# One-bank instead of two-bank PSUM tiles in the second layer, and a fold's seven combinations beside one tile

## The chip, the cores and the metric

One core of a Trainium2 chip runs the whole program. The metric is device time in microseconds; the kernel before takes 1497.6 us, the median of 3 runs (1495.95 to 1499.32).

## The reference

```
attention twice, per batch and head: packed = attn(p, k, v); x = attn(q, packed, packed)
    B = 8, H = 8, S = 576, head 64, 32 packed tokens;  x becomes 4608 x 512
xn  = x / rms(x) * rms_g
y   = (silu(xn @ w_gate) * (xn @ w_val)) @ w_out      512 -> 1536 -> 512
a, b = y @ w1, y @ w2                                 512 -> 1024 each
out = ((a * b) @ w3) @ w_out2                         1024 -> 1024 -> 512
```

Inputs and outputs are 32-bit floats.

## The kernel before

Every 32-bit operand of a matmul is split into two parts, a rounded high part and the rest (`split`, L54 to L56: ScalarE copies, VectorE or GpSimd subtracts), and each product is made as three matmuls: high by high, high by low, low by high. 

The program runs in stages. Attention and the dense gate and value layer come first and leave the activations transposed in device memory (hT_d). Then nine *y tiles* of 512 tokens each multiply them by w_out (`y_part`, L549 to L568). A y tile has 12 steps; in each, SP issues the load of a slice hr four steps ahead, ScalarE and VectorE split a slice two steps ahead into hh and hl, and TensorE does 12 matmuls into four PSUM banks. At the end four evictions and two stores (y_d) follow. Tiles alternate between two sets of banks, "gv" and "at".

Beside the y tiles run two other pieces of work, cut into small steps by Python generators. `fold_parts` (L665 to L695) takes w3 @ w_out2, which `folded` has made on TensorE into the tiles w34o, and makes seven combinations of its four blocks: each is one `put`, that is a ScalarE copy and a VectorE subtraction of 128 x 1024 and a store, some with additions on GpSimd. `layer2` (L634 to L642) rounds the blocks of w1 and w2 (`converting`; c_h and c_y are ScalarE's copies, lines 108 and 109) and makes seven combinations of each of four groups (`group`), stored to ws_d. `together` (L407 to L420) spreads such generators over the steps of the y tiles: each has a number of calls, and a start and an end as shares of the stage; at most one call, that of the one furthest behind, goes with each step, and whatever is left of a generator is run at the end in one go. Stores are held back by some steps (`store_later`, `stores`, L349 to L356) and issued on SP, in whose queue the loads of hr stand as well. `fetch_y` loads the first token block for the second layer.

The second layer works on five pairs of token blocks, three of 512 and two of 384 tokens wide. Each 2 x 2 block product is made by a scheme of seven products instead of eight, so that one step has 7 products x 6 = 42 matmuls, into four accumulators ta, tb, tc and td (`step`, L841 to L890). The order of the products is ta, tb, tc, then ta, tb again, td, tc again. In between, ScalarE copies ta to p1 (a tile named hr, L867), VectorE makes u2 and u3 from tb and p1, c22 from tc and u3, s1 from td and u3 times ta, and the last u2 from tc (the helper `dve` at L839; u2 and c22 are the two halves of a tile named uc, s1 is a tile named s), and GpSimd multiplies u2 by c22 (L883) and makes differences. A pair has 8 steps. Even steps put the four accumulators in four one-bank tiles "gv", odd steps in two two-bank tiles "at", ta and tb in the first, tc and td in the second:

```
def slot(tag):                                                   # L48
    return ps.tile([128, 2, 512], F32, tag=tag, name=tag, bufs=2)
def bank():                                                      # L51
    return ps.tile([128, 512], F32, tag="gv", name="gv", bufs=4)
def four(tag):
    if tag == "gv":
        return [bank() for _ in range(4)]
    return [t[:, j, :] for t in (slot("at"), slot("at")) for j in range(2)]
```

After the 8 steps of a pair comes its output product (`run`, L915 to L985): 28 units of 6 matmuls (L951), each unit three matmuls into the accumulators `acc[0]` in "gv" and three into `acc[1]` in "at", with the same seven-product scheme and the same VectorE and ScalarE reads between. Weights come in tiles of 1024 or 768 KB with four buffers; taking one issues the load of the next (`load_w`, `next_w`, L748 on, issue at L756). All eight PSUM banks are in use: four for "gv", four for "at". The order of instructions on an engine is the order in which the program writes them; tiles and semaphores decide only who waits.

Of the kernel before, what the change touches and what calls it, by code (L numbers as in the profile page):

```python
# [8 lines left out]
F32 = mybir.dt.float32  # L9
# [23 lines left out]
def packed_attention_swiglu_bilinear(ctx: ExitStack, tc, qT, kT, v, pT, rms_g, w_gv, w_out,  # L33
                                     w1, w2, w3T, w_out2, out):
    nc = tc.nc
    PSUM = bass.MemoryType.PSUM
# [8 lines left out]
    y_d = dram.tile([NT // TT, 128, 4, TT], F32, name="y_d")  # L45
    ws_d = [dram.tile([8, 128, 2, n, 2, 128], F32, name=f"ws{n}_d") for n in (3, 4)]

    def slot(tag):  # L48
        return ps.tile([128, 2, 512], F32, tag=tag, name=tag, bufs=2)

    def bank():  # L51
        return ps.tile([128, 512], F32, tag="gv", name="gv", bufs=4)
# [346 lines left out]
    def some(gen, n):  # L399
        for _ in range(n):  # L400
            yield next(gen, None)
# [5 lines left out]
    def together(main, total, *others, most=1):  # L407


        done, taken = 0.0, [0] * len(others)  # L410
        for c in main:
            done += c / total
            late = [n * (done - a) / (z - a) - taken[i] if taken[i] < n else 0.0
                    for i, (n, _, a, z) in enumerate(others)]
            for i in sorted(range(len(others)), key=lambda j: -late[j])[:most]:
                if late[i] > 0:
                    next(others[i][1], None)
                    taken[i] += 1
        for _, gen, _, _ in others:
            drain(gen)  # L420
# [128 lines left out]
    def y_part(t, tag):  # L549
        acc = four(tag)  # L550
        for kk in range(NF):
            n = NF * t + kk
            fetch_h(n + 4)
            split_h(n + 2)
            hi, lo = hts.pop(n)
            for m in range(4):
                for a, (w, x) in enumerate(((wo_h, hi), (wo_h, lo), (wo_l, hi))):
                    nc.tensor.matmul(acc[m], lhsT=w[:, kk, 128 * m:128 * m + 128], rhs=x,  # L558
                                     start=(kk == 0 and a == 0), stop=(kk == NF - 1 and a == 2))
            if kk < NF - 1:  # L560
                stores()
                yield 1.0
        for h in range(2):
            y = yp.tile([128, 2, TT], F32, tag="y", name="y", bufs=2)
            for m in range(2):
                evict(y[:, m], acc[2 * h + m], m)
            store_later(3, out=y_d[t, :, 2 * h:2 * h + 2], in_=y)
        yield 1.0  # L568
# [141 lines left out]
    def fetch_y(p):  # L710
        if p < len(pairs):
            ys[p] = []
            row, w = pairs[p]
            for r in (row, row + w):
# [8 lines left out]

    second = layer2()
    third = fold_parts()
    together(y_part(4, "at"), 12.0, (6, some(second, 6), 0.5, 1.0), (5, some(third, 5), 0.0, 0.9))
    together(chained(y_part(5, "gv"), y_part(6, "at"), y_part(7, "gv")), 36.0, (31, second, 0.0, 0.9),
             (3, third, 0.0, 0.15),
             (1, (fetch_y(0) for _ in range(1)), 0.3, 0.4))

    flush()
# [93 lines left out]
             (3, first_w(), 0.3, 0.8))  # L825
    flush()
    wo_ctx.close()
    p3 = ctx.enter_context(tc.tile_pool(name="p3", bufs=1, side="left"))
    sides = {n: p3.tile([128, 4, TT], F32, name=n) for n in ("s11", "s21", "s12", "s22", "t1s", "t2s", "t4s")}
    OPER = {0: "s11", 4: "t1s", 5: "t2s", 1: "s21", 6: "s12", 3: "t4s", 2: "s22"}  # L830
# [10 lines left out]
    def step(p, n):  # L841
        w = width(p)
        i = LAYER[n]
        half, k = divmod(i, 4)
        xh, xl = xs[p]

        def side(name):
            return sides[name][:, k, :w]

        def prod(t, j, start):  # L850
            pos = ORDER.index(j)
            wi, pos, n = (wa, pos, 3) if pos < 3 else (wb_, pos - 3, 4)
            wi = wi[:, :512 * n].rearrange("p (r j s n) -> p r j s n", r=2, j=n, s=2)
            at = 0
            for a, x in ((0, xh), (1, xh), (0, xl)):
                for r in range(2):
                    nc.tensor.matmul(t, lhsT=wi[:, r, pos, a], rhs=x[:, j, r, :w],  # L857
                                     start=(start and at == 0), stop=(at == 5), skip_group_check=True)
                    at += 1

        ta, tb, tc_, td = (t[:, :w] for t in four("at" if n % 2 else "gv"))
        p1, u3, uc = tmp()[:, :w], tmp()[:, :w], two()
        u2, c22 = uc[:, 0, :w], uc[:, 1, :w]
        s1, s2 = (side("s21"), side("s22")) if half else (side("s11"), side("s12"))
        wa = next_w()
        prod(ta, 0, True)
        nc.scalar.activation(out=p1, in_=ta, func=AF.Copy)  # L867
        prod(tb, 5, True)
        dve(u2, tb, p1)
        prod(tc_, 4, True)  # L870
        yield
        wb_ = next_w()
        prod(ta, 1, False)
        prod(tb, 6, False)
        dve(u3, tb, p1)
        dve(c22, tc_, u3)
        yield
        prod(td, 3, True)
        dve(s1, td, u3)
        dve(s1, s1, ta, ALU.mult)  # L880
        prod(tc_, 2, False)
        dve(u2, tc_, u2)
        nc.gpsimd.tensor_tensor(out=s2, in0=u2, in1=c22, op=ALU.mult)  # L883
        if half == 0:
            diff(side("t1s"), s2, s1, nc.gpsimd)
        else:
            diff(side("t2s"), s2, side("t1s"), nc.gpsimd)
            diff(side("s12"), s2, side("s12"), nc.gpsimd)
            diff(side("t4s"), s1, side("t2s"), nc.gpsimd)
        yield  # L890
# [24 lines left out]
    def run(p):  # L915
        w = width(p)
        ahead = splitting(p, AHEAD)
        diffs = early(p + 1)
        for n in range(8):
            for part, _ in enumerate(step(p, n)):  # L920
                if part in EARLY.get(n, ()):
                    next(ahead)
                if n == 1 and part == 0:
                    fetch_y(p + 1)
                if n in (4, 5) and part == 1:
                    next(diffs, None)
        xs.pop(p)
        drain(ahead)
        drain(diffs)
        later = splitting(p, LATER)  # L930
        sum_ = sums(p + 1)
        acc = [[t[:, :w] for t in four(tag)] for tag in ("gv", "at")]
        p1, u2, u3, c22 = [], [], [], []
        out_stores = []

        def keep(m, half, side, o):
            out_stores.append(dict(out=out[256 * half + 128 * m:256 * half + 128 * m + 128,
                                           pairs[p][0] + side * w:pairs[p][0] + side * w + w], in_=o))

        BANK = {0: 0, 1: 0, 5: 1, 6: 1, 4: 2, 2: 2, 3: 3}  # L940
        for a, j in enumerate(PROD):
            wi = next_w().rearrange("p (s i n) -> p s i n", s=2, i=4)
            last = {0: 1, 5: 6, 4: 2}.get(j, j) == j
            for k in range(4):
                for _ in range(ISSUE[4 * a + k]):
                    next(later, None)
                hi, lo = his.pop((j, k))
                for m in range(2):
                    t = acc[m][BANK[j]]
                    for n, (s, x) in enumerate(((0, hi), (1, hi), (0, lo))):  # L950
                        nc.tensor.matmul(t, lhsT=wi[:, s, k, 128 * m:128 * m + 128], rhs=x,  # L951
                                         start=(j in (0, 5, 4, 3) and k == 0 and n == 0),
                                         stop=(k == 3 and n == 2), skip_group_check=True)
                if k == 1:
                    next(sum_, None)
                if out_stores:
                    nc.sync.dma_start(**out_stores.pop(0))
            for m in range(2):
                ta, tb, tc_, td = acc[m]
                if j == 0:  # L960
                    p1.append(tmp()[:, :w])
                    nc.scalar.activation(out=p1[m], in_=ta, func=AF.Copy)
                elif j == 5:
                    uc = two()
                    u2.append(uc[:, 0, :w])
                    c22.append(uc[:, 1, :w])
                    dve(u2[m], tb, p1[m])
                elif j == 1:
                    c11 = tmp()[:, :w]
                    nc.scalar.activation(out=c11, in_=ta, func=AF.Copy)  # L970
                    keep(m, 0, 0, c11)
                elif j == 6:
                    u3.append(tmp()[:, :w])
                    dve(u3[m], tb, p1[m])
                    dve(c22[m], tc_, u3[m])
                    keep(m, 1, 1, c22[m])
                elif j == 3:
                    dve(u3[m], td, u3[m])
                    keep(m, 1, 0, u3[m])
                elif j == 2:  # L980
                    dve(u2[m], tc_, u2[m])
                    keep(m, 0, 1, u2[m])
        drain(sum_)
        for x in out_stores:
            nc.sync.dma_start(**x)  # L985
# [34 lines left out]
```

## Time and profile before

| | |
|---|---|
| median of 3 runs | 1497.6 us |
| the profiled execution | 1496.0 us |
| its span, first to last instruction | 1494.2 us |
| mean granted TensorE clock | 0.984 |
| TensorE busy | 1360.8 us, 91% |
| VectorE busy | 871.6 us, 58% |
| ScalarE busy | 576.5 us, 39% |
| GpSimd busy | 607.0 us, 41% |
| the nine y tiles and the folding end, and layer 2 starts, at | 865.5 us |

A busy share is the share of the span in which the engine worked on an instruction. The granted clock is the part of full speed at which TensorE was allowed to run: 1.00 is 2.4 GHz, 0.5 is 1.2 GHz.

### The profile page before, as it was taken

Reading aid. Unit: us, or ns where it says so; the run is one execution under the profiler, and the core shown is the slowest. Engines: PE = TensorE matmul, PEld = TensorE weight load, DVE = VectorE, ACT = ScalarE, POOL = GpSimd, SP = SyncE. Lnnn points to the kernel's source line nnn. Section 1 sums busy time; section 2 is a strip of 40 time slices with the busy share of each in tenths; the row PEclk is TensorE's granted clock in tenths of the full one; section 3 lists DMA queues with packets and bytes.
Section 4 is the critical chain, followed back from the end, with each engine's and each line's share of the span. In section 5 each row is a group of like instructions: output and inputs, shape, how many; then the busy total and the mean of one; then the engine's idle time right before and its main releaser. Section 6 shows DMA issues by size and latency. Waiting matters only on the chain.

```text
span 1494.2 us, 23206 instructions
## 1 busy us (share of the span) xinstructions
PE 1360.8 (91%) x8800; PEld 1119.2 (75%) x8800; DVE 871.6 (58%) x1356; ACT 576.5 (39%) x1141; POOL 607.0 (41%) x524
## 2 busy tenths in 40 slices
PE   4579999999999999999899998998889889988888
PEld 2368888888888888888788776776667667878778
DVE  4786576676675577364786734654573447346344
ACT  3465554554556665252555410240042015014013
POOL 2455544545555622022344232452335326235233
PEclk9689999999999999999999999999999999999999
DMA  9844544433213577344899764465447545756654
GB/s 298 302 172 129 188 145 155 160 121 125 104 72 131 182 262 241 100 159 132 309 349 395 261 230 150 169 213 224 155 169 238 178 162 190 269 205 223 226 211 155
DMA packets 82080, 293.55 MB, mean 196 GB/s; under 512 B 9008, under 2 KB 14128, under 8 KB 68016
## 3 DMA queue, kind: packets, MB, share of 16 engines
q1 hardware_dynamic: 81968, 292.07, 56.4%
q8 instruction: 69, 1.13, 0.3%
q14 instruction: 43, 0.35, 0.1%
HBM read 219.68 MB, written 72.35 MB: 195 GB/s over the span
## 4 chain that ended last, share of the span: by engine, by line
PE 72%; DVE 13%; ACT 4%; DMA 3%; issue 3%; SPq 1%; POOL 0%; DVEq 0%; ACTq 0%; POOLq 0%
PE gv L376 17%; PE at L857 12%; PE gv L857 10%; PE at L558 9%; PE at L951 5%; PE gv L951 5%; PE gv L558 4%; PE gv L654 3%; DVE hr L839 3%; DVE uc L839 2%; PE at L337 2%; DMA w<-in_w_dram 1%; DMA hr<-hT_d 1%; PE at L292 1%; DVE s L839 1%
## 5 line engine op out<-in xcount | busy, mean ns | idle before, releaser
L388 POOL TENSOR_TENSOR ht<-th,vl 128x288 f32<-128x288 f32 x192 | 163.6, 861 | 166.7 <-ACT vl L387 79.3
L857 PE MATMUL at<-xh,w 128*128 128x512 f32 (+1 forms) x560 | 146.2, 383 | 56.1 <-DVE uc L839 28.1
L376 PE MATMUL gv<-ah,wbh 128*128 128x288 f32 x768 | 178.0, 313 | 7.3 <-DVE th L383 4.7
L883 POOL TENSOR_TENSOR s<-uc 128x512 f32<-128x512 f32 (+1 forms) x40 | 48.5, 1214 | 313.8 <-DVE uc L839 313.8
L376 PE MATMUL gv<-al,wbh 128*128 128x288 f32 x768 | 166.8, 298 | 0.0
L857 PEld LDWEIGHTS at<-xh,w 128*128 128x128 f32 x560 | 98.9, 189 | 90.2 <-DVE uc L839 35.7
L376 PEld LDWEIGHTS gv<-ah,wbh 128*128 128x128 f32 x768 | 122.3, 190 | 58.5 <-issue 22.8
L376 PE MATMUL gv<-ah,wbl 128*128 128x288 f32 x768 | 165.0, 296 | 0.0
L114 POOL TENSOR_TENSOR c_o<-c_o,c_y 128x512 int32<-128x512 int32 x52 | 74.4, 1431 | 173.0 <-DVE c_o L112 152.3
L857 PE MATMUL gv<-xh,w 128*128 128x512 f32 (+1 forms) x560 | 140.4, 372 | 3.4 <-DVE uc L839 2.2
L56 DVE TENSOR_TENSOR hl<-hr,hh 128x512 fp32r<-128x512 f32 x108 | 98.9, 919 | 49.5 <-ACT hh L55 49.3
L376 PEld LDWEIGHTS gv<-al,wbh 128*128 128x128 f32 x768 | 124.7, 190 | 1.0 <-DVE al L56 0.6
L376 PEld LDWEIGHTS gv<-ah,wbl 128*128 128x128 f32 x768 | 124.3, 190 | 0.0
L857 PEld LDWEIGHTS gv<-xh,w 128*128 128x128 f32 x560 | 101.4, 188 | 23.5 <-DVE uc L839 11.0
L383 DVE SCALAR_TENSOR_TENSOR th<-th,gv 128x288 f32<-128x288 f32 x192 | 84.4, 445 | 55.9 <-ACT th L382 52.1
L558 PE MATMUL at<-hl,wo_h 128*128 128x512 f32 x288 | 112.6, 391 | 2.3 <-DVE hl L56 2.3
L558 PE MATMUL at<-hh,wo_h 128*128 128x512 f32 x288 | 112.4, 390 | 0.2 <-ACT hh L55 0.2
L558 PE MATMUL at<-hh,wo_l 128*128 128x512 f32 x288 | 112.3, 390 | 0.0
L55 ACT ACTIVATE hh<-hr 128x512 fp32r<-128x512 f32 x108 | 67.5, 628 | 97.1 <-PE at L558 49.9
L387 ACT ACTIVATE vl<-gv 128x288 f32<-128x288 f32 x192 | 79.5, 414 | 62.1 <-PE gv L376 58.5
L56 DVE TENSOR_TENSOR wbl<-at,wbh 128x512 fp32r<-128x512 f32 x96 | 66.0, 687 | 61.2 <-ACT wbh L55 60.6
L951 PE MATMUL at<-sh,w 128*128 128x512 f32 (+1 forms) x280 | 83.9, 381 | 13.1 <-DVE uc L839 12.4
(148 smaller groups left out, 2828.0 us busy)
## 6 DMA issues: line engine op xcount, KB each, us to landing
w<-ws_d SPq DMA_DIRECT2D x40, 1024.0 KB, 4.8
w<-w_d SPq DMA_DIRECT2D x35, 1024.0 KB, 4.8
w<-ws_d SPq DMA_DIRECT2D x40, 768.0 KB, 4.4
hT_d<-ht SPq DMA_DIRECT2D x96, 288.0 KB, 2.6
hr<-hT_d SPq DMA_DIRECT2D x108, 256.0 KB, 5.3
w<-in_w_gv_dram SPq DMA_DIRECT2D x24, 512.0 KB, 7.2
w<-in_w_out_dram SPq DMA_DIRECT2D x20, 512.0 KB, 4.8
v<-in_v_dram SPq DMA_DIRECT2D x8, 1152.0 KB, 8.1
```

Source lines behind the costliest of these rows:

```text
L55: nc.scalar.activation(out=hi, in_=src, func=AF.Copy)
L56: eng_lo.tensor_tensor(out=lo, in0=src, in1=hi.bitcast(F32), op=ALU.subtract)
L114: nc.gpsimd.tensor_tensor(out=d, in0=d, in1=shape(y), op=ALU.add)
L376: nc.tensor.matmul(t[:, :HALF], lhsT=w[:, e, 256 * i + 128 * f:256 * i + 128 * f + 128], rhs=x[:, e, HALF * hf:HALF * hf + HALF], start=(n ...
L383: nc.vector.scalar_tensor_tensor(out=th, in0=th, scalar=1.0, in1=t[:, :HALF], op0=ALU.add, op1=ALU.mult)
L387: nc.scalar.activation(out=vl, in_=t[:, :HALF], func=AF.Copy, scale=0.5)
L388: nc.gpsimd.tensor_tensor(out=ht[:, hf], in0=th, in1=vl, op=ALU.mult)
L558: nc.tensor.matmul(acc[m], lhsT=w[:, kk, 128 * m:128 * m + 128], rhs=x, start=(kk == 0 and a == 0), stop=(kk == NF - 1 and a == 2))
L839: nc.vector.tensor_tensor(out=out, in0=a, in1=b, op=op)
L857: nc.tensor.matmul(t, lhsT=wi[:, r, pos, a], rhs=x[:, j, r, :w], start=(start and at == 0), stop=(at == 5), skip_group_check=True)
L883: nc.gpsimd.tensor_tensor(out=s2, in0=u2, in1=c22, op=ALU.mult)
L951: nc.tensor.matmul(t, lhsT=wi[:, s, k, 128 * m:128 * m + 128], rhs=x, start=(j in (0, 5, 4, 3) and k == 0 and n == 0), stop=(k == 3 and n ...
```

## The change

The two-bank "at" tiles move to a PSUM pool of their own, which is closed after the last y tile; from then on the same four banks are four one-bank tiles, for the odd steps of the second layer and for the second accumulator group of the output product. And all seven combinations of the folded weight are made beside the fifth y tile (`y_part(4, ...)`), where five were before and two beside the sixth to eighth.

```diff
+    slots_ctx = ExitStack()
+    slots = slots_ctx.enter_context(tc.tile_pool(name="slots", bufs=1, space=PSUM))
+
     def slot(tag):
-        return ps.tile([128, 2, 512], F32, tag=tag, name=tag, bufs=2)
+        return slots.tile([128, 2, 512], F32, tag=tag, name=tag, bufs=2)
...
-    together(y_part(4, "at"), 12.0, (6, some(second, 6), 0.5, 1.0), (5, some(third, 5), 0.0, 0.9))
+    together(y_part(4, "at"), 12.0, (6, some(second, 6), 0.5, 1.0), (7, third, 0.0, 0.9))
     together(chained(y_part(5, "gv"), y_part(6, "at"), y_part(7, "gv")), 36.0, (31, second, 0.0, 0.9),
-             (3, third, 0.0, 0.15),
              (1, (fetch_y(0) for _ in range(1)), 0.3, 0.4))
...
     wo_ctx.close()
+    slots_ctx.close()
+    pt = ctx.enter_context(tc.tile_pool(name="pt", bufs=1, space=PSUM))
+
+    def banks(n):
+        if n % 2:
+            return [pt.tile([128, 512], F32, tag="at", name="at", bufs=4) for _ in range(4)]
+        return four("gv")
...
-        ta, tb, tc_, td = (t[:, :w] for t in four("at" if n % 2 else "gv"))
+        ta, tb, tc_, td = (t[:, :w] for t in banks(n))
...
-        acc = [[t[:, :w] for t in four(tag)] for tag in ("gv", "at")]
+        acc = [[t[:, :w] for t in banks(m)] for m in range(2)]
```

In the changed kernel L857 is L867, L839 is L849, L951 is L961, L55 is L58, L356 is L359 and L489 is L492.

On TensorE, an odd step of the second layer, from the second product (tb) on; at_9896 holds ta and tb, at_9897 tc and td, and w is the weight tile. Before:

```order
L857 MATMUL at_9896<-xh_9645,w_9799 128x512 [waits Activation_49]
L857 MATMUL at_9896<-xh_9645,w_9799 128x512 x3
L857 MATMUL at_9896<-xl_9646,w_9799 128x512 x2
L857 MATMUL at_9897<-xh_9645,w_9799 128x512 x4
L857 MATMUL at_9897<-xl_9646,w_9799 128x512 x2
L857 MATMUL at_9896<-xh_9645,w_9841 128x512 [waits DMAHW1_49,DVE_49]
L857 MATMUL at_9896<-xh_9645,w_9841 128x512 x3
L857 MATMUL at_9896<-xl_9646,w_9841 128x512 x2
L857 MATMUL at_9896<-xh_9645,w_9841 128x512 x4
L857 MATMUL at_9896<-xl_9646,w_9841 128x512 x2
L857 MATMUL at_9897<-xh_9645,w_9841 128x512 [waits DVE_49]
L857 MATMUL at_9897<-xh_9645,w_9841 128x512 x3
```

The same step after, from the third product (tc, at_9905) on; ta is at_9903, tb at_9904, td at_9906:

```order
L867 MATMUL at_9905<-xh_9648,w_9802 128x512 x4
L867 MATMUL at_9905<-xl_9649,w_9802 128x512 x2
L867 MATMUL at_9903<-xh_9648,w_9848 128x512 [waits DMAHW1_49,Activation_49]
L867 MATMUL at_9903<-xh_9648,w_9848 128x512 x3
L867 MATMUL at_9903<-xl_9649,w_9848 128x512 x2
L867 MATMUL at_9904<-xh_9648,w_9848 128x512 [waits DVE_49]
L867 MATMUL at_9904<-xh_9648,w_9848 128x512 x3
L867 MATMUL at_9904<-xl_9649,w_9848 128x512 x2
L867 MATMUL at_9906<-xh_9648,w_9848 128x512 x4
L867 MATMUL at_9906<-xl_9649,w_9848 128x512 x2
L867 MATMUL at_9905<-xh_9648,w_9848 128x512 [waits DVE_49]
L867 MATMUL at_9905<-xh_9648,w_9848 128x512 x3
```

The matmuls stand in the same order. The wait of tb for ScalarE's copy of ta is gone from the second product and stands at the fourth, ta's own second use; td no longer waits. The even steps ("gv") have had these waits all along.

On ScalarE, the seam between the fifth and the sixth y tile (hh is the high part of an hr slice, stage the place of a combination, c_o a rounded block of w1, w34o a folded block). Before:

```order
L55 ACTIVATE hh<-hr 128x512
L547 ACTIVATE y<-at 128x512 x2
L108 ACTIVATE c_h<-w_8586 128x512
L109 ACTIVATE c_y<-w_8586 128x512
L55 ACTIVATE stage_6931<-c_o 128x4x128
L55 ACTIVATE stage_6932<-w34o_7939 128x1024
L55 ACTIVATE hh<-hr 128x512
L55 ACTIVATE stage_6931<-c_o 128x4x128
L55 ACTIVATE hh<-hr 128x512
L55 ACTIVATE stage_6932<-w34o_7939 128x1024
L55 ACTIVATE hh<-hr 128x512
```

After:

```order
L58 ACTIVATE hh<-hr 128x512
L550 ACTIVATE y<-at 128x512 x2
L111 ACTIVATE c_h<-w_8563 128x512
L112 ACTIVATE c_y<-w_8563 128x512
L111 ACTIVATE c_h<-w_8592 128x512
L112 ACTIVATE c_y<-w_8592 128x512
L58 ACTIVATE stage_6934<-c_o 128x4x128
L58 ACTIVATE stage_6935<-w34o_8362 128x1024
L58 ACTIVATE hh<-hr 128x512
L58 ACTIVATE stage_6934<-c_o 128x4x128
L58 ACTIVATE hh<-hr 128x512
L58 ACTIVATE stage_6934<-c_o 128x4x128 x2
```

One rounding of a block more stands between the evictions and the next hh, and one copy out of w34o instead of two stands among the next hh's.

On SP's queue, the end of the eighth y tile (ws_d are the stores of the last group of combinations, w the first weight load of layer 2). Before:

```order
L489 DMA hr<-hT_d 128x512 x5
L356 DMA ws_d<-stage_6932 128x768
L356 DMA ws_d<-stage_6932 128x1024
L356 DMA ws_d<-stage_6932 128x768
L356 DMA ws_d<-stage_6932 128x1024
L356 DMA ws_d<-stage_6932 128x768
L356 DMA ws_d<-stage_6932 128x1024
L356 DMA ws_d<-stage_6932 128x768
L356 DMA ws_d<-stage_6932 128x1024
L356 DMA y_d<-y 128x1024 x2
L489 DMA hr<-hT_d 128x512 x5
```

After:

```order
L492 DMA hr<-hT_d 128x512 x5
L359 DMA ws_d<-stage_6935 128x768
L359 DMA ws_d<-stage_6935 128x1024
L492 DMA hr<-hT_d 128x512
L359 DMA ws_d<-stage_6935 128x768
L359 DMA ws_d<-stage_6935 128x1024
L492 DMA hr<-hT_d 128x512
L359 DMA ws_d<-stage_6935 128x768
L359 DMA ws_d<-stage_6935 128x1024
L359 DMA ws_d<-stage_6935 128x768
L359 DMA ws_d<-stage_6935 128x1024
L359 DMA y_d<-y 128x1024 x2
```

The eight stores stood in one block; now loads of hr stand between them. The steps of `layer2` take places 0 to 31 of the three y tiles (but for one that goes to `fetch_y`, at place 12 instead of 21), where they ended at place 34.

## Rows read from the trace of the kernel before

**Rows 1.** The chain that ended last: share of the span by engine.

```profile
PE 72%; DVE 13%; ACT 4%; DMA 3%; issue 3%; SPq 1%; POOL 0%; DVEq 0%; ACTq 0%; POOLq 0%
```

**Rows 2.** Groups of instructions: busy us, mean ns | idle us before, and what ended it.

```profile
L857 PE MATMUL at<-xh,w 128*128 128x512 f32 (+1 forms) x560 | 146.2, 383 | 56.1 <-DVE uc L839 28.1 <-DVE s L839 14.6 <-ACT hr L867 13.5
L857 PE MATMUL gv<-xh,w 128*128 128x512 f32 (+1 forms) x560 | 140.4, 372 | 3.4 <-DVE uc L839 2.2
L951 PE MATMUL at<-sh,w 128*128 128x512 f32 (+1 forms) x280 | 83.9, 381 | 13.1 <-DVE uc L839 12.4
```

**Rows 3.** Timeline of TensorE, wide steps: start us, us, engine, line, instruction [idle before].

```profile
875.57 1.09 PE L857 MATMUL at<-xh,w 128*128 128x512 f32 x4
...
885.05 1.20 PE L857 MATMUL at<-xh,w 128*128 128x512 f32 x4 [1.51 <-DVE uc L839]
...
887.49 1.20 PE L857 MATMUL at<-xh,w 128*128 128x512 f32 x4 [0.78 <-DVE s L839]
...
888.99 1.07 PE L857 MATMUL gv<-xh,w 128*128 128x512 f32 x4
...
1220.27 1.09 PE L857 MATMUL at<-xh,w 128*128 128x512 f32 x4
...
1233.76 0.63 PE L951 MATMUL gv<-sh,w 128*128 128x512 f32 x2
```

**Rows 4.** Timeline of TensorE, narrow steps (first and last of them).

```profile
1276.03 0.86 PE L857 MATMUL gv<-xh,w 128*128 128x384 f32 x4
...
1283.81 0.85 PE L857 MATMUL at<-xh,w 128*128 128x384 f32 x4
...
1294.43 0.86 PE L857 MATMUL gv<-xh,w 128*128 128x384 f32 x4
...
1446.26 0.85 PE L857 MATMUL at<-xh,w 128*128 128x384 f32 x4
...
1457.87 0.84 PE L951 MATMUL gv<-sh,w 128*128 128x384 f32 x2
```

**Rows 5.** Timeline of TensorE in an output product.

```profile
990.00 0.39 PE L951 MATMUL gv<-sl,w 128*128 128x512 f32 x1
991.82 0.73 PE L951 MATMUL at<-sh,w 128*128 128x512 f32 x2 [1.43 <-DVE uc L839]
992.39 0.40 PE L951 MATMUL at<-sl,w 128*128 128x512 f32 x1
```

**Rows 6.** Timeline of ScalarE and TensorE, seam of the fifth and sixth y tile.

```profile
724.07 0.66 ACT L108 ACTIVATE c_h<-w 128x512 f32<-128x512 f32 x1 [1.02 <-DMA w<-in_w_dram]
...
727.46 0.39 PE L558 MATMUL gv<-hh,wo_l 128*128 128x512 f32 x1
...
732.90 0.80 PE L558 MATMUL gv<-hl,wo_h 128*128 128x512 f32 x1 [2.88 <-DVE hl L56]
...
733.92 0.63 PE L558 MATMUL gv<-hh,wo_h 128*128 128x512 f32 x1
...
738.62 0.52 PE L558 MATMUL gv<-hh,wo_l 128*128 128x512 f32 x1
```

**Rows 7.** Timeline of SP's queue and TensorE, seam of the eighth and ninth y tile.

```profile
826.77 7.32 SPq L356 DMA_DIRECT2D ws_d<-stage  x8
...
839.51 0.50 PE L558 MATMUL at<-hl,wo_h 128*128 128x512 f32 x1 [1.76 <-DVE hl L56]
```

**Rows 8.** Windows: us, busy PE, PEld, DVE, ACT, POOL (count), PEclk, DMA share, GB/s.

```profile
888.99:898.94 9.95, 9.80 (x43) 7.81 (x42) 5.81 (x7) 1.12 (x2) 5.53 (x4) 1.00 0.52 184
1096.49:1140.08 43.59, 40.40 (x169) 31.38 (x168) 29.58 (x30) 22.18 (x33) 28.98 (x16) 1.00 0.58 192
1276.00:1350.00 74.00, 63.19 (x339) 57.97 (x338) 30.74 (x57) 6.40 (x14) 21.02 (x20) 1.00 0.66 235
1446.26:1457.87 11.61, 9.07 (x44) 8.09 (x44) 4.28 (x8) 1.73 (x4) 2.02 (x2) 0.91 0.53 182
```

**Rows 9.** DMA issues: KB each, median us from issue to landing.

```profile
w<-ws_d SPq DMA_DIRECT2D x40, 1024.0 KB, 4.8
```

## The prediction

> **What bounds the kernel now.** I read the chain of waits first: TensorE holds 72% of the path to the last instruction and VectorE another 13%, while DMA has 3% [rows 1]. So I looked next at where TensorE waits for VectorE, in the groups by line and tile. The reader should compare the two matmul groups of layer 2: 560 matmuls into "gv" tiles were preceded by 3.4 us of idle time, and 560 of the same kind into "at" tiles by 56.1 us. The matmuls of the output product into "at" lost another 13.1 us [rows 2]. Same operands, same order, same number; the tile differs. The timeline of TensorE then shows it step by step: the odd step from 875.57 to 888.99 takes 13.42 us [rows 3], the even step after it 9.95 [rows 8]. Inside that odd step TensorE sits still for 1.51 us before the matmuls at 885.05, until VectorE has made uc, and for 0.78 us before those at 887.49, until VectorE has made s [rows 3]; the third wait, for ScalarE's copy hr, is in the group row: 13.5 us over the 20 odd steps, 0.68 each [rows 2].
>
> Why only there: an "at" tile holds two banks, ta with tb and tc with td. A matmul into tb waits for ScalarE's copy out of ta; the next one into ta waits for VectorE's read of tb; td waits for a read of tc, tc for a read of td. None of these is an overlap of data: they are reads of the other half of the same tile. The even steps have the same arithmetic in four tiles and wait only for a read of the same bank, which by then is long past: 3.4 us in 20 steps.
>
> **The change part by part.** (1) *Odd steps of layer 2.* The order of the matmuls stays; in the instruction order the waits of an odd step become word for word those of an even one. ScalarE's copy is now waited for two products later, and the waits for td after tc and tc after td go or move to a read of the same bank. Nothing else is added, since four banks of "at" existed before. So I price an odd step at what its neighbour costs, which also includes the slow restart after each stall. Wide pairs (512 tokens): 12 odd steps, 13.42 for one of the first (875.57 to 888.99) and 13.49 for the last (1220.27 to 1233.76), against 9.95 [rows 8]. I take 3.46 us each: 12 x 3.46 = 41.5. Narrow pairs (384): 8 odd steps; 10.62 (1283.81 to 1294.43) against 7.78 (1276.03 to 1283.81), so 2.84 each, 7 x 2.84 = 19.9; the last one took 11.61 (1446.26 to 1457.87) [rows 4], 3.83 more than 7.78, since its granted clock fell near its end, to 0.91 as the mean of the step [rows 8]. Sum 41.5 + 19.9 + 3.8 = **65.2 us**. Bounds: at best the last waits of a step, which even steps still have, go as well (3.4 us over 20 steps in the gv row [rows 2], so 68.6); at worst only the idle time of the row, 56.1, comes back.
>
> (2) *Output product.* It keeps one accumulator group in "at". The same false pairing stalls it at four places in each of the five products (counted in the timeline); the rows show one: between 990.00 and 991.82 there is one matmul of 0.23 us and 1.43 us of idle time, and the two at 991.82 take 0.57 to the next where 0.46 would be the pitch (0.23 each, a little under the even step's mean of 9.95 / 42 = 0.237) [rows 5]. So a stall costs 1.82 - 0.23 + 0.11 = 1.70 us for 1.43 idle: some 0.27 us of restart beside the idle time. All idle time of that group, 13.1 [rows 2], plus 20 restarts of 0.27 gives 13.1 + 5.4 = **18.5 us**. Nothing hides a stall: the matmuls into the other accumulators, in "gv", stand behind the waiting one on the same engine. Bounds: 13.1 below, 18.5 above; half of it if VectorE turns out to be busy at those places (below).
>
> (3) *The fold's seven combinations.* Before, five of seven came beside the fifth y tile (one of them drained at its end) and three calls (two real combinations and an empty one) beside the next three; now all seven come beside the fifth, one drained at its end. Per moved combination: one ScalarE copy, one VectorE subtraction, one store on SP's queue. At the seam of the fifth and sixth y tile TensorE already starves: from 727.46 to 732.90 two matmuls ran where 5.44 us fit 24, and from 733.92 to 738.62 eleven matmuls took 0.427 each, against 0.23 at the higher clock level [rows 6]. That is 5.0 + 0.6 + 11 x 0.2 = 7.8 us lost, since the drained work stands ahead of hh on ScalarE's queue and ahead of hl on VectorE's. After the change one conversion more is drained there (two ScalarE operations of 0.66 [rows 6]), and one combination instead of two stands there. I take +1 us; bounds -8 (the stall goes) and +8 (it doubles). The second place is the seam of the eighth and ninth tile: eight stores of ws hold SP for 7.32 us and the five hr loads queue behind them; TensorE then waits 1.76 us at 839.51 [rows 7], and about as much again follows in smaller gaps. With three steps freed, layer 2's preparation ends three steps earlier, and the stores are spread, with hr loads between them. I take -2.5; bounds 0 and -3.3. The load of the first token block is issued some nine steps earlier; it lands under the same y tiles: 0, bounds -1 and +1. With +0.5 for denser work beside the fifth tile, part 3 is **-1 us**, from -11 to +5.
>
> *The pools.* Closing one PSUM pool and opening another makes the first odd step wait for the last y tile's matmuls and evictions; a whole even step of 10 us lies between, which hides them. Without that cover it would be about one eviction, under 1 us.
>
> Sum: 65.2 + 18.5 + 1 = 84.7 us. The profiled execution took 1496.0 us (span 1494.2), 1.6 below the median of the runs, 1497.6, and inside their spread. 1496.0 - 84.7 = 1411.3; on the median it is 1412.9. I say 1412, between the two.
>
> What is late next? In an even step of 9.95 us VectorE is busy 5.81 and GpSimd 5.53 [rows 8], so a row of even steps leaves both 40% free. In a product of 43.59 us VectorE is busy 29.58 and GpSimd 28.98 [rows 8]; in 39.9 us that is 74% and 73%, tight but not full. Weights: each step takes a 1024 KB and a 768 KB load, and the larger lands in a median of 4.8 us [rows 9]; with four buffers a load is issued about 1.4 steps ahead, 11 us in a narrow step of 7.78. The DMA share in a narrow pair would rise from 0.66 over 74 us [rows 8] to 0.66 x 74 / 62.5 = 0.78.
>
> **Rivals.** *A: the change does nothing.* If the waits stayed (by tag instead of by tile), 1496 to 1498. Against it: in the order of the changed kernel the waits stand where the gv steps have them. Chance 0.02.
>
> *B: something else binds in the odd steps.* With TensorE faster, VectorE's chain u2, u3, c22, s1 or the weight loads might be late, and half of part 1 goes into new waits: 84.7 - 32.6 = 52.1, so 1444 in the profile, 1446 as a median. For it: VectorE and GpSimd are near three quarters in the products, DMA near 0.78 in narrow pairs. Against it: an even step already runs at 9.95 us directly behind the leftovers of an odd one. Chance 0.06.
>
> *C: slower, by the clock.* The odd steps now also go round four single banks. If short waits between products made TensorE's granted clock fall to the lower level there, a matmul would take 0.427 instead of 0.23 [rows 6]: 42 x 0.2 = 8.4 us in a wide odd step, 6.3 in a narrow one (three quarters), 12 x 8.4 + 8 x 6.3 = 151 us in all. That gives 1496.0 - 84.7 + 151 = 1562; it decides from some 11 of 20 odd steps at the lower level on (84.7 / 7.55). Against it: the even step at 888.99 already does just this, with a granted clock of 1.00, and the odd step's longer idle times were granted 1.00 as well, over the 74 us of four narrow step pairs [rows 8]; the fall at 733 came after 5 us of nearly no work, and the last odd step's dip stands behind its stalls. Chance 0.02.
> The Trainium skill speaks for C: its page "TensorE: Matmul & The Clock Gate", section "A second HAM failure mode: psum-queue depth-cycling", tells of a kernel whose going round PSUM banks left TensorE short idle times between groups, so that its clock swung between the levels and throughput fell. By that rule the sum would be C's; by the rows it is mine, since here the four-bank steps are the ones with the least idle time.
>
> **How the numbers follow.** Forecast 0.90, A 0.02, B 0.06, C 0.02. For the forecast's own ends: best 68.6 + 18.5 + 11 = 98, worst 56.1 + 9.2 - 5 = 60; all terms at one end together is not likely, so for 8 in 10 I take 1401 to 1428, which leaves B and C outside. A measurement of this kernel tells about 0.2% (3 us) from no change. Faster: forecast and B, 0.96; same: A, 0.02; slower: C, 0.02.
>
> **What would show it.** In the profile after: "at" and "gv" matmul groups of layer 2 with like idle times (each under 6 us); odd steps of 10.0 and 7.8 us; a product of about 40 us in place of 43.6; TensorE's share of the span near 96%; the seam at 727 still there. Wrong, if odd steps stay above 11 us with VectorE or a DMA as the releaser (B), or the granted clock falls below 0.95 behind 860 us (C).

## The result and the profile after

The changed kernel takes 1410.28 us, the median of 4 runs (1408.94 to 1411.63), against 1498.4 for the kernel before beside it: a ratio of 0.9414, 95% interval 0.9398 to 0.9431. The forecast was 1412, with a range of 1401 to 1428. The profiled execution's span fell from 1494.2 to 1409.8 us, by 84.4; the sum was 84.7.

The chain of waits in the changed kernel, as in [rows 1]:

```profile
PE 79%; DVE 10%; ACT 3%; issue 2%; DMA 1%; POOL 1%; SPq 0%; DVEq 0%; ACTq 0%; POOLq 0%
```

VectorE's share of the chain fell from 13% to 10%. The groups of TensorE's matmuls, in the columns of [rows 2] (L867 was L857, L961 was L951, L849 was L839):

```profile
L867 PE MATMUL gv<-xh,w 128*128 128x512 f32 (+1 forms) x560 | 140.5, 372 | 3.5 <-DVE uc L849 2.5
L867 PE MATMUL at<-xh,w 128*128 128x512 f32 (+1 forms) x560 | 140.4, 372 | 3.4 <-DVE uc L849 2.5
...
L961 PE MATMUL at<-sh,w 128*128 128x512 f32 (+1 forms) x280 | 81.7, 373 | 0.0
```

"at" and "gv" can no longer be told apart in the steps: 3.4 us of idle time against 3.5, where "at" had 56.1 [rows 2]. In the products the "at" matmuls had waited 13.1 us and wait no more.

The timeline of TensorE through an odd step of the changed kernel, which answers to [rows 3]:

```profile
873.94 1.07 PE L867 MATMUL at<-xh,w 128*128 128x512 f32 x4
875.30 1.07 PE L867 MATMUL at<-xh,w 128*128 128x512 f32 x4
...
880.74 1.07 PE L867 MATMUL at<-xh,w 128*128 128x512 f32 x4
882.41 1.19 PE L867 MATMUL at<-xh,w 128*128 128x512 f32 x4 [0.15 <-DVE uc L849]
883.91 1.07 PE L867 MATMUL gv<-xh,w 128*128 128x512 f32 x4
```

Products follow each other every 1.36 us, and only the last, tc's second, waits for VectorE: a true wait, for c22. The windows of that step, of a wide output product, of a narrow odd step and of four pairs of narrow steps, columns as in [rows 8]:

```profile
873.94:883.91 9.97, 9.82 (x44) 7.81 (x42) 4.09 (x6) 0.60 (x1) 2.58 (x2) 1.00 0.87 350
1063.10:1102.45 39.35, 39.35 (x169) 31.64 (x168) 27.90 (x31) 22.17 (x33) 29.27 (x16) 1.00 0.63 208
1245.08:1252.87 7.79, 7.59 (x43) 7.27 (x43) 3.25 (x6) 0.49 (x1) 2.03 (x2) 1.00 0.70 258
1221.75:1283.95 62.20, 60.61 (x338) 58.01 (x336) 30.25 (x56) 6.41 (x14) 21.05 (x20) 1.00 0.78 283
```

The odd step went from 13.42 to 9.97 us, the product from 43.59 [rows 8] to 39.35 with no idle time of TensorE, the narrow odd step from 10.62 [rows 4] to 7.79, all at a granted clock of 1.00. DMA is at 0.78 in the narrow pairs, and nothing there waits for it.

At the seam of the fifth and sixth y tile it went the other way; this timeline of TensorE answers to [rows 6]:

```profile
727.61 0.39 PE L561 MATMUL gv<-hh,wo_l 128*128 128x512 f32 x1
733.21 0.80 PE L561 MATMUL gv<-hh,wo_h 128*128 128x512 f32 x1 [5.21 <-ACT hh L58]
736.57 0.79 PE L561 MATMUL gv<-hl,wo_h 128*128 128x512 f32 x1 [2.57 <-DVE hl L59]
737.16 0.63 PE L561 MATMUL gv<-hh,wo_l 128*128 128x512 f32 x1
```

Two matmuls take 8.96 us from 727.61 to 736.57, and over the next ones, to 741.43, the granted clock is 0.50, the lower level. Added up from what each start is later than the pitch (the 0.23 us from one start to the next), the seam costs 11.2 us, against 7.9 before. After it, up to layer 2, the changed kernel has no gap at all, where the one before had 4.7 us of them, the wait at 839.51 [rows 7] among them. The stretch from the first matmul of the fifth y tile to the first of layer 2 went from 175.97 us (689.57 to 865.54) to 174.61 (689.32 to 863.93).

### The profile page after: what moved, and what is told of

Same layout as the page of the kernel before. It is cut to its first block, busy times and chain, and to the rows that moved or that the text cites. A ratio compares the mean times of both kernels' runs of the same rounds, so it can differ in the third digit from the quotient of the medians.

```text
span 1409.8 us, 23211 instructions
## 1 busy us (share of the span) xinstructions
PE 1341.5 (95%) x8800; PEld 1121.0 (80%) x8800; DVE 866.6 (61%) x1356; ACT 576.2 (41%) x1141; POOL 612.2 (43%) x524
## 4 chain that ended last, share of the span: by engine, by line
PE 79%; DVE 10%; ACT 3%; issue 2%; DMA 1%; POOL 1%; SPq 0%; DVEq 0%; ACTq 0%; POOLq 0%
PE gv L379 18%; PE at L561 12%; PE at L867 11%; PE gv L867 11%; PE gv L561 7%; PE gv L961 6%; PE at L961 6%; PE gv L657 3%; PE at L340 2%; DVE uc L849 2%; DVE hr L849 2%; DMA hr<-hT_d 1%; PE at L295 1%; DVE th L386 1%; ACT th L385 1%
## 5 line engine op out<-in xcount | busy, mean ns | idle before, releaser
L117 POOL TENSOR_TENSOR c_o<-c_o,c_y 128x512 int32<-128x512 int32 x52 | 73.4, 1412 | 176.7 <-DVE c_o L115 164.9
L867 PE MATMUL gv<-xh,w 128*128 128x512 f32 (+1 forms) x560 | 140.5, 372 | 3.5 <-DVE uc L849 2.5
L867 PE MATMUL at<-xh,w 128*128 128x512 f32 (+1 forms) x560 | 140.4, 372 | 3.4 <-DVE uc L849 2.5
L867 PEld LDWEIGHTS gv<-xh,w 128*128 128x128 f32 x560 | 101.2, 188 | 24.1 <-DVE uc L849 11.4
L867 PEld LDWEIGHTS at<-xh,w 128*128 128x128 f32 x560 | 101.4, 188 | 23.5 <-DVE uc L849 11.0
L386 DVE SCALAR_TENSOR_TENSOR th<-th,gv 128x288 f32<-128x288 f32 x192 | 84.4, 445 | 56.1 <-ACT th L385 52.9
L58 ACT ACTIVATE hh<-hr 128x512 fp32r<-128x512 f32 x108 | 67.6, 628 | 95.1 <-PE at L561 44.9
L385 ACT ACTIVATE th<-gv 128x288 f32<-128x288 f32 x192 | 79.4, 413 | 41.5 <-PE gv L379 41.4
```

Source lines behind the costliest of these rows:

```text
L58: nc.scalar.activation(out=hi, in_=src, func=AF.Copy)
L117: nc.gpsimd.tensor_tensor(out=d, in0=d, in1=shape(y), op=ALU.add)
L385: nc.scalar.activation(out=th, in_=t[:, :HALF], func=AF.Tanh, scale=0.5)
L386: nc.vector.scalar_tensor_tensor(out=th, in0=th, scalar=1.0, in1=t[:, :HALF], op0=ALU.add, op1=ALU.mult)
```

## The experiments

The theory to test: TensorE waited for reads of the other bank of the same tile, and nothing else made the odd steps long. Its rivals: the two-bank tile costs by itself, whoever shares it; or the fold's move carries part of the gain. Times are medians; each ratio is against the kernel before in the same session.

**One half of the change each.** The first keeps the old spreading of the fold, the second keeps the two-bank tiles:

```diff
 k1_tiles_only: the changed kernel with
-    ... (6, some(second, 6), 0.5, 1.0), (7, third, 0.0, 0.9))
+    ... (6, some(second, 6), 0.5, 1.0), (5, some(third, 5), 0.0, 0.9))
+             (3, third, 0.0, 0.15),
 k2_fold_only: the kernel before with those lines the other way round
```

> The changed kernel with the old spreading of the fold's combinations, so the one-bank tiles alone. Theory (waits on the other half of a two-bank tile made the difference; the fold's move is worth 1.6 us): 1412 us, layer 2 as in the changed kernel (odd steps 10.0 and 7.8 us), the seam at 727 us costs 8 us of TensorE again and the seam at 837 us 3.5. Rival (the shorter preparation brings a good part of the gain): well above 1420 us.

> The kernel before with the new spreading of the fold's combinations alone; the two-bank tiles stay. Theory: 1497 us, 1.6 less than before, which a measurement can't tell from nothing; in its trace the seam at 727 us costs 11 us instead of 8, the gaps at 801 and 837 us are gone, and the odd steps take 13.4 and 10.6 us. Rival (the preparation brings a good part): below 1485 us.

The tiles alone: 1411.3 us, ratio 0.9432 (0.9413 to 0.9451). The fold alone: 1493.47 us, ratio 0.9979 (0.9965 to 0.9993). So the tiles are the change. The fold's move is small; the runs put it at 0.07 to 0.35%, that is 1 to 5 us where 1.6 were expected, and the traces at the lower end of that: with the tiles alone the stretch of y tiles takes 175.90 us, as before, and loses 7.6 us at the first seam and 4.9 behind it; with the fold alone it takes 174.31, loses 10.9 at the seam and nothing behind. The two costs come with the schedule, in the traces of before, k1, k5 and k6 on one side and of the changed kernel, k2, k3 and k4 on the other, and nearly cancel.

**Other partners in the same two-bank tiles.** The kernel before, with one line of `step` changed:

```diff
-        ta, tb, tc_, td = (t[:, :w] for t in four("at" if n % 2 else "gv"))
 k5_pair_ad_bc
+        ta, td, tb, tc_ = (t[:, :w] for t in four("at" if n % 2 else "gv"))
 k6_pair_ac_bd
+        ta, tc_, tb, td = (t[:, :w] for t in four("at" if n % 2 else "gv"))
```

> The kernel before, two-bank tiles kept, but ta shares its tile with td and tb with tc in the odd steps. Theory (who shares decides): the only wait added to an even step's is that of tc's first product for VectorE's u2, one operation after tb: 0.78 us idle as for s in the kernel before, and 0.27 of restart, so 11.0 us in a wide odd step and 8.7 in a narrow one; 1498.4 - 65.4 + 20 = 1453 us. Rival (a two-bank tile costs by itself, in the banks): no change, 13.4 us a step and 1498 us.

> As the last one, but ta shares with tc and tb with td. Theory: td then waits for u3, one VectorE operation after tb (0.78 us idle), and tc's second product for s1 times ta, two operations after td (about 1.5), each with 0.27 of restart, and the last 0.45 of an even step falls away: 12.4 us in a wide odd step, 9.9 in a narrow one; 1498.4 - 65.4 + 45 = 1478 us, between the other pairings. Rival (a two-bank tile costs by itself): 1498 us.

Measured: 1452.32 us, ratio 0.971 (0.9688 to 0.9733), and 1475.65 us, ratio 0.9862 (0.9841 to 0.9882), where 1453 and 1478 were expected. The timeline of TensorE in an odd step of k5, then of k6:

```profile
874.76 1.07 PE L857 MATMUL at<-xh,w 128*128 128x512 f32 x4
877.12 1.21 PE L857 MATMUL at<-xh,w 128*128 128x512 f32 x4 [0.84 <-DVE uc L839]
878.63 1.09 PE L857 MATMUL at<-xh,w 128*128 128x512 f32 x4
```

```profile
875.76 1.07 PE L857 MATMUL at<-xh,w 128*128 128x512 f32 x4
877.12 1.07 PE L857 MATMUL at<-xh,w 128*128 128x512 f32 x4
878.48 1.07 PE L857 MATMUL at<-xh,w 128*128 128x512 f32 x4
880.79 1.21 PE L857 MATMUL at<-xh,w 128*128 128x512 f32 x4 [0.78 <-DVE hr L839]
883.96 1.20 PE L857 MATMUL at<-xh,w 128*128 128x512 f32 x4 [1.50 <-DVE s L839]
```

In k5 the one new wait stands before tc, for u2, a read of its neighbour tb. In k6 it is td that waits for u3 (the tile hr), a read of tb, and tc that waits for the second of the two operations on s, which reads ta. The wide odd step takes 11.14 to 11.20 us in k5 and 12.40 to 12.44 in k6. Same tiles, same banks, same matmuls: the partner alone sets the step between 11.2 and 13.4. The rival of the two-bank tile that costs by itself is out. And ta's neighbour tc hears of ScalarE's copy of ta in k6 too, at 875.76, without a wait: one product, 1.36 us, in between was enough for that one operation.

**Steps and products apart.** The changed kernel, with a pool opened and closed around the steps and around the product of each pair, and one-bank tiles in one of them only (the last line is that of k3; k4 has one-bank tiles there):

```diff
 k3_steps_ones: steps four tiles of [128, 512]; product two of [128, 2, 512]
 k4_product_ones: steps two of [128, 2, 512]; product four of [128, 512]
+        open_pool("ls")
         ahead = splitting(p, AHEAD)
...
+        open_pool("lp")
+        acc = [[t[:, :w] for t in x] for x in (four("gv"), twos())]
```

> The changed kernel, but the second accumulator group of the output products is in two-bank tiles again (the pool is opened and closed for each pair). Theory: the products take 43.6 us (wide) again, the steps stay at 10.0 and 7.8; 1410.3 + 17.8 = 1428 us. Rival (product stalls were VectorE's lateness, not the pairing): products stay near 39.4 us and the time near 1410.

> The other way round: two-bank tiles in the odd steps, one-bank tiles in the products. Theory: odd steps 13.4 and 10.6 us, products 39.4; 1410.3 + 65.4 = 1476 us, and the two gains add up to the whole. Rival (they overlap): below 1465.

Measured: 1427.84 us, ratio 0.9532 (0.9514 to 0.955), and 1478.97, ratio 0.9873 (0.9853 to 0.9894). With one-bank steps the wide products take 43.65, 43.64 and 42.68 us; with one-bank products, 39.7. The first product of k3, the stall in it that answers to [rows 5] (in the kernel of k3, L971 is the product's matmul and L857 the helper `dve`), and the first product of k4:

```profile
943.28:986.93 43.65, 40.66 (x169) 31.24 (x168) 29.28 (x31) 22.06 (x33) 29.23 (x16) 1.00 0.59 192
```

```profile
974.12 0.39 PE L971 MATMUL gv<-sl,w 128*128 128x512 f32 x1
975.94 0.73 PE L971 MATMUL at<-sh,w 128*128 128x512 f32 x2 [1.43 <-DVE uc L857]
```

```profile
957.97:997.67 39.70, 39.62 (x170) 31.57 (x168) 27.68 (x30) 22.07 (x33) 29.43 (x16) 1.00 0.63 206
```

The losses against the whole change, 17.6 and 68.7 us, add to 86.3, close to the 88.1 between the medians of before and after: the two parts do not overlap. k4 is 3 us over its expectation. In its trace four narrow steps at a lower granted clock (last section) cost some 3.0 us over their like, where the kernel before had one such step, of 0.9; and its five products together take 1.6 us more than in the changed kernel.

**The seam.** What is left over at the end of the fifth y tile is taken away: four steps of `layer2` there instead of six, and 33 instead of 31 later.

```diff
-    ... (6, some(second, 6), 0.5, 1.0), (7, third, 0.0, 0.9))
-    ... (31, second, 0.0, 0.9),
+    ... (4, some(second, 4), 0.3, 1.0), (7, third, 0.0, 0.7))
+    ... (33, second, 0.0, 0.9),
```

> The changed kernel, with four steps of the second layer's preparation beside the fifth y tile instead of six, so that nothing is left to be run in one go at its end; 33 instead of 31 go beside the next three. Theory (the seam's 11 us of TensorE are the work left over in front of hh and hl): the stall at 727 us goes, 1410.3 - 11 = 1399 us, less if the preparation, now ending two steps later, brings back the gap at 837 us (3.5). Rival (the seam waits for the loads of hr behind the stores on SP): the stall stays and so does the time.

Measured: 1408.02 us (1407.31 to 1408.8), ratio 0.9401 (0.938 to 0.9421); 2.3 us won, not 11: the expectation was missed. The waits of TensorE in the y tiles of k7, after them those of the changed kernel:

```profile
PE at L561 <- DVE hl L59: 3.2, 7, 1.0
PE gv L561 <- DVE hl L59: 0.8, 2, 0.6
PE at L561 <- ACT hh L58: 0.6, 1, 0.6
PE gv L561 <- ACT hh L58: 0.6, 1, 0.6
```

```profile
PE gv L561 <- ACT hh L58: 5.2, 1, 5.2
PE gv L561 <- DVE hl L59: 2.6, 1, 2.6
```

The long stall did go, but eleven short ones came; by gaps they cost 3.1 us before 720 us and 6.1 behind, so the stretch fell only from 174.61 to 172.89. The seven combinations now crowd into nine steps, four of them in a row, and most of the new waits are for VectorE's hl.

**The order of the products.** A step still took 9.97 us for 42 matmuls. Two lines change places:

```diff
+        prod(tb, 6, False)
         prod(ta, 1, False)
-        prod(tb, 6, False)
```

> The changed kernel with the fourth and fifth product of a step exchanged: tb's second before ta's second. Theory (the 0.45 us by which a step is longer than its 42 matmuls is tc's wait for c22, two VectorE operations after tb's second product with one product between): with two products between the wait goes, 40 steps x 0.45 = 18 us, 1392 us. Rival (tb's second product then waits for u2, of which there is only one product between): the wait moves and the time stays at 1410 or grows.

Measured: 1393.12 us (1392.84 to 1396.05), ratio 0.9304 (0.9285 to 0.9323). Groups of k8, then the same places of its timeline:

```profile
L867 PE MATMUL gv<-xh,w 128*128 128x512 f32 (+1 forms) x560 | 138.2, 368 | 2.3 <-DVE uc L849 2.2
L867 PE MATMUL at<-xh,w 128*128 128x512 f32 (+1 forms) x560 | 137.7, 367 | 0.0
```

```profile
871.01 1.07 PE L867 MATMUL at<-xh,w 128*128 128x512 f32 x4
...
879.17 1.07 PE L867 MATMUL at<-xh,w 128*128 128x512 f32 x4
...
1212.63 0.97 PE L867 MATMUL gv<-xh,w 128*128 128x384 f32 x4 [0.80 <-DVE uc L849]
```

The seven products of a wide step follow each other without a gap, 9.52 us. The rival is right in the first step of the two narrow pairs (8.39 us from 1208.51, and 8.95 in the other, against 7.30): there tb does wait for u2, 2.2 us in all.

**Both, and the seam better spread.** k9 is k7 and k8 together; k10 spreads the combinations evenly; k11 leaves one rounding at the seam:

```diff
 k9_seam_swap
+    ... (4, some(second, 4), 0.3, 1.0), (7, third, 0.0, 0.7))    and 33 later
 k10_even_swap
+    ... (4, some(second, 4), 0.1, 0.9), (7, third, 0.0, 0.9))    and 33 later
 k11_five_swap
+    ... (5, some(second, 5), 0.2, 1.0), (7, third, 0.0, 0.9))    and 32 later
```

> The exchanged products and the preparation of four steps beside the fifth y tile together. If the two are independent: 1393.1 less the 2.3 that the second gave alone, 1391 us; TensorE loses about 9 us in the y tiles, in many gaps under 1.5 us, as it did with the second alone. If the earlier small gaps were chance: 1385.

> As the last one, but the seven combinations stand evenly among the twelve steps of the fifth y tile (steps 0, 2, 3, 5, 6, 8, 10) and not in its first nine; the roundings at 1, 4, 7, 9. Theory (the new gaps between 700 and 720 us are VectorE's 2.2 us subtractions in four steps running, against a step of 2.73): the 3 us lost there go, 1388 us. Rival (it is the loads of hr, late in a stretch where the DMA engines are busy 0.86 of the time): 1391 as before.

> Five steps of the preparation beside the fifth y tile: one rounding still stands at the seam behind the evictions, but nothing that waits for it (no combination of the second layer and none of the fold's) is in front of hh. Theory (the seam's 11 us are ScalarE held by the copy that waits for the rounding's way over VectorE and GpSimd, not the rounding's own 1.3 us): the seam costs under 3 us, 1384 to 1387. Rival (any work left over at the seam costs it): 8 us or more stay, 1390 and up.

Measured: 1394.38 us, ratio 0.9318 (0.9305 to 0.9331); 1391.87, ratio 0.9299 (0.9287 to 0.9312); 1391.47 (1389.13 to 1392.84), ratio 0.9294 (0.9281 to 0.9307). All three lie above what was expected (1391, 1388, and 1384 to 1387), and k10 and k11 where the rivals put them. k9 wins nothing on k8, and k10 and k11 are the lowest of the study, though their intervals overlap k8's: that they are faster than k8 is not shown by the times. The traces do tell them apart. The stretch of y tiles takes 174.28 us in k8, 174.12 in k9, 170.76 in k10 and 169.60 in k11. The 3 us lost before 720 us are gone in k10, which speaks for VectorE's crowded subtractions there; the DMA engines were no freer (busy 0.94 of 690 to 725 us, against 0.86 in k9), which speaks against late loads. And in k11, where a rounding stands at the seam but nothing that waits for it is in front of hh, the seam costs 2.4 us instead of 10.4 in k8. TensorE's two longest waits at k11's seam:

```profile
723.95 0.50 PE L561 MATMUL gv<-hh,wo_h 128*128 128x512 f32 x1 [0.74 <-ACT hh L58]
724.67 0.50 PE L561 MATMUL gv<-hl,wo_h 128*128 128x512 f32 x1 [0.22 <-DVE hl L59]
```

The times show less of this than the stretches do: the stages before differ by up to 2 us from trace to trace (the fifth y tile starts at 687.16 in k8, 689.20 in k11), and the profiled executions of k10 and k11, 1389.72 and 1389.13 us, are the fastest of their runs.

## Why the prediction was right

*Odd steps, 65.2 us forecast.* The twelve wide ones took 161.3 us and take 119.9, the eight narrow ones 86.2 and now 62.3: 41.4 + 23.9 = 65.3 us. The step of the argument that carried it was to price an odd step by its even neighbour in the same trace rather than by its idle time alone (56.1), which leaves out the restart after each stall. k5 and k6 show why it was right: what a wait costs goes by which operation reads the partner, and by how many products lie between.

*Products, 18.5 us.* 43.57, 43.59, 42.27 and 33.43 us became 39.36, 39.35, 39.35 and 30.01, and the last won 3.0 between its first and last matmul: 17.8 in all. With 13.1 us of idle time [rows 2] that leaves 0.24 a stall for the restart, where 0.27 were taken from one of them. The 1.43 us of idle time at 991.82 [rows 5] was a false wait: it is gone in the changed kernel, and k3 has it again.

*Fold and y tiles, -1 us.* The stretch changed by -1.36, but both terms in it were wrong. The seam was put at +1 (and +0.5 beside the tile) and became 3.3 dearer; the second seam was put at -2.5 and its gaps, with the smaller ones before it, went altogether, -4.7. That the two errors nearly cancel, so that the sum came out, was luck. The term that failed is "one conversion more ... two ScalarE operations of 0.66": it priced the extra rounding by its time on ScalarE. ScalarE, GpSimd and VectorE at the seam of the changed kernel:

```profile
723.80 0.63 ACT L58 ACTIVATE hh<-hr 128x512 fp32r<-128x512 f32 x1 [3.06 <-DMA hr<-hT_d]
...
725.29 0.66 ACT L111 ACTIVATE c_h<-w 128x512 f32<-128x512 f32 x1
...
726.97 0.66 ACT L112 ACTIVATE c_y<-w 128x512 int32<-128x512 uint32 x1
...
729.76 1.26 POOL L117 TENSOR_TENSOR c_o<-c_o,c_y 128x512 int32<-128x512 int32 x1 [0.69 <-DVE c_o L115]
731.05 0.63 ACT L58 ACTIVATE stage<-c_o 128x512 fp32r<-128x512 f32 x1 [3.43 <-POOL c_o L117]
...
732.54 0.61 ACT L58 ACTIVATE hh<-hr 128x512 fp32r<-128x512 f32 x1
732.66 2.18 DVE L59 TENSOR_TENSOR stage<-w34o,stage 128x1024 fp32r<-128x1024 f32 x1 [0.26 <-ACT stage L58]
```

The copy of c_o at 731.05 stands in front of hh and waits until the rounding has passed VectorE and GpSimd: ScalarE is idle for 3.43 us with hh behind it in its queue. VectorE's subtraction for the fold's combination, 2.18 us, then stands in front of hl. Part of the delay is not the rounding's: ScalarE had waited 3.06 us for a load of hr before the evictions, so that the first rounding starts at 725.29 and not at 724.07 as before [rows 6]. k11 keeps a rounding at the seam and has neither that copy nor the fold's combination in front of the seam's first hh and hl, and the seam falls to 2.4 us; what each of the two costs by itself was not tried.

*The rivals.* A is out: the waits went with the tiles. B is out: the odd steps have no new waits (3.4 us of idle time in all, and 9.97 us a step, as in the even ones), and in a product, where VectorE is busy 27.90 of 39.35 us and GpSimd 29.27, TensorE has no gap. That there was room for more is shown by k8, which takes 17 us more out of the steps. C is out: all odd steps run at a granted clock of 1.00.

The three measured parts, 65.3 + 17.8 + 1.4 = 84.5 us, account for the 84.4 by which the span fell.

## What to carry to other kernels

Compare groups of the same instruction that differ only in the tile: a difference in idle time with the same operands points at sharing, and the price of removing it is the neighbour's time, restart included. If the banks must be shared, choose partners so that few reads of the one stand right in front of a matmul into the other (k5, with one such place in a step instead of three, gave 45 us for one line). A piece of work left in front of a critical one can cost the way over other engines that it waits for (3.43 us of idle ScalarE here), and not only its own time on the queue (0.63).

## What the runs showed of the hardware beside this

In four of the five kernels with two-bank odd steps (before, k2, k4 and k6) the granted clock fell in one or two narrow odd steps and in the even step right behind, where there was one. In k5, which has one stall in an odd step instead of two or three, and in the kernels with one-bank odd steps it fell in none, in one trace of each. Windows of an odd step, the even one behind it and a later odd one of k4:

```profile
1272.22:1283.68 11.46, 8.99 (x43) 8.03 (x43) 3.34 (x6) 0.49 (x1) 2.00 (x2) 0.92 0.91 319
1283.68:1292.14 8.46, 8.26 (x44) 7.94 (x43) 3.98 (x7) 0.90 (x2) 4.27 (x4) 0.91 0.62 222
...
1378.18:1389.71 11.53, 9.06 (x43) 8.09 (x43) 3.34 (x6) 0.49 (x1) 2.02 (x2) 0.91 0.49 174
```

Each such step took some 0.6 to 0.9 us more than its like; in every case the fall came near the end of an odd step, about its last stall. The kernel before shows it in its last odd step [rows 8], k4 in four steps, k2 in three, k6 in two. Over the whole of layer 2's steps the changed kernel, k1, k3 and k5 were granted 1.00. What starts a fall in one stalled step and not in the next stays open; it was not tried.

The Trainium skill's page "TensorE: Matmul & The Clock Gate", section "A second HAM failure mode: psum-queue depth-cycling", puts such swings of the clock down to short idle times between groups in a kernel that cycles through PSUM banks. The short idle times agree with these traces, where the falls stand at stalls (0.91 above). Going round banks is not enough for it here: the kernels in which every step goes round four single banks were granted 1.00 in all of layer 2's steps.
